# Block attention and routed experts on one core: another order of the attention steps, block means in a score bank, three subtractions on GpSimd

## The chip, the cores and the metric

The kernel runs on one core of a Trainium2 chip. Times are microseconds (us) of the device, from the first to the last instruction of the program and the little that lies around them. The engines are named as the profile names them: PE is TensorE, DVE is VectorE, ACT is ScalarE, POOL is GpSimd and SP is SyncE; PEld is PE's loading of weights.

## What is computed

```python
def _attn_ref(q, k, v):                      # 4 batches, 8 heads, 768 positions, 64 wide
    block, window = (32, 16)
    k_sum = k.reshape(B, H, nb, block, D).max(axis=3)
    v_sum = v.reshape(B, H, nb, block, D).mean(axis=3)
    scores_l = scale * np.matmul(q, k.transpose(0, 1, 3, 2))
    mask_l = np.abs(pos[:, None] - pos[None, :]) < window
    scores_s = scale * np.einsum('bhsd,bhnd->bhsn', q, k_sum) + np.log(block)
    scores_all = np.concatenate([np.where(mask_l, scores_l, -1e9), scores_s], axis=-1)
    a = np.exp(scores_all - np.max(scores_all, axis=-1, keepdims=True))
    a = a / (np.sum(a, axis=-1, keepdims=True) + 1e-09)
    return np.matmul(a, np.concatenate([v, v_sum], axis=2))

def reference(...):
    x = attention output, 3072 tokens of 512
    return _moe_ref(x, ...)                  # each token: 1 of 4 groups, 1 of its 4 experts,
                                             # relu(x @ w1) @ w2, weighted
```

Each query sees its 31 nearest keys, and 24 block keys (the maximum over 32 keys) with 24 block values (the mean over 32). The result is routed to one of 16 experts for each token.

## The kernel before

**Attention.** It runs over 16 pairs of heads, `idx` (4 pairs in each of 4 batches), and each pair has 3 steps, g = 0, 1, 2, so that step n = 3 idx + g; 48 steps in all. Every engine works through its instructions in the order in which the program is written, and that order is a table written by hand: `PLAN` (L49) lists for each g the pieces that a step is made of, and `START` (L52) the first four steps. The pieces:

- `s` (`scores`, L781): 8 fp32 matmuls of queries (64 rows) by the 120 keys of a tile, for 2 heads. PE runs them on quarters of its array, 64 by 64. Two of the three `ps_s` banks take the result. DVE adds the mask and takes the minimum (`ss`, `nm`, L795).
- `e` (L804): four exponentials on ACT, into `pr`.
- `t` (L807): four transposes of `pr` from two steps back, on the whole array into a bank of `ps_tr` (there are three); ACT copies them to `ptS` (L812).
- `v` (`values`, L815): 8 matmuls of `ptS` from three steps back with the values, on halves of the array (121 by 64), into the one bank `ps_av`; DVE divides (`rs`, `xt`, L826 and L827).
- `p0` to `p4` (`prep`, L742): for the next pair. `p0` and `p1` transpose the keys `kn` of head 0 and 1 (whole array, `ps_tr`) and copy them to `kw` in two halves (L764): the first half by ACT, the second by DVE, or by ACT too for head 1 from pair 10 on (`ACT_K1`). `p2` and `p3` transpose the queries `qn`, and ACT copies them to `qt` (L758). `p4` is DVE alone: the keys at the edges of each tile (L772, L773), the block maxima `ks` (L775), and their copy into `kw` (L778).
- `m0`, `m1` (`means`, L721): the block means of the values. `m0` is 12 matmuls with `stair` on quarters by columns (96 by 32) for the next pair, `m1` one matmul with `same` for this pair (128 by 25); both into a bank of `ps_tr`. DVE copies both (`vp` L731, `vr` L735), and POOL spreads `vr` into the values `va` (L738, six copies).
- `l0` to `l3`: transposes and matmuls (`xt`, `wcat`, 128 by 32) of the finished pair for the routing logits.
- `w`: four matmuls on zeros that keep PE busy (`keep_warm(4)`).

The scores of the next pair need all of `kw` and `qt`. Between the pieces, `advance` puts the router's small operations into DVE's stream (tokens to experts): 1 after each `s`, 2 after each `v`, 2 within `p4`, from step 17 on.

**The crossing to the experts.** Hooks in `block_attention_then_moe` start the first expert in the last steps. The first expert's weights are loaded as fp32 and split into a high part (ACT, L1035) and a low part, the difference (a DVE subtraction of 128x1024), in four pieces each for `w1` and `w2` (`split_w`, L1022). In step 47 `x_t1` transposes the first gathered tokens `xg` into two banks of `ps_tr`, from which ACT and DVE make `xT`. POOL starts the gathers of tokens and the load of `w2`. Matmuls of the experts then fill PE to the end.

Of the kernel before, what the change touches and what calls it, by code (L numbers as in the profile page):

```python
# [45 lines left out]
EPS = 1e-9  # L46
NEG = -1.0e9

PLAN = [["s", "p0", "l1", "t", "v", "p1", "e", "p4"],  # L49
        ["s", "p2", "t", "v", "m1", "l2", "e"],  # L50
        ["s", "p3", "l3", "t", "v", "l0", "m0", "e"]]
START = [["s", "e"], ["s", "m0", "e"], ["s", "w", "t", "m1", "p0", "p1", "e", "p4", "p2", "p3"],  # L52
         ["t", "v", "s", "n0", "p0", "p1", "e", "p4"]]
LAG = {"l0": 1, "l1": 2, "l2": 2, "l3": 2}

T_LAG, V_LAG = 2, 3
# [10 lines left out]
FIRST = {1: 2, 2: 1, 3: 1}  # L67

XT_AT = 4


AHEAD, LATE_AHEAD, SLOT_AHEAD, WEIGHT_AHEAD, VECTOR_NS = 300, 1500, 800, 3000, 85
# [517 lines left out]
def attention(tc, q, k, v, w_group, w_expert, ident, x_dram, ps, router, hook):  # L590
# [24 lines left out]
    with ExitStack() as st, ExitStack() as nat_st:  # L615
# [105 lines left out]
        def means(idx, part):  # L721

            va = va_ring[idx % NVA]
            t = ps_tr.next()
            if part == 0:
                for i in range(NQT):
                    j = i % 4
                    T.matmul(out=t[32 * j:32 * j + 32, 0:P], lhsT=stair[:, NBLK - 2 - 2 * i:NBLK + 30 - 2 * i],
                             rhs=va[0:KW, i, :, 0:D], start=(i < 4), stop=(i >= NQT - 4), skip_group_check=True)
                vps[idx] = sm.tile([P, P], F32, name="vp", bufs=2)  # L730
                V.tensor_copy(out=vps[idx], in_=t[:, 0:P])  # L731
            else:
                T.matmul(out=t[KW:NR, 0:P], lhsT=same, rhs=vps.pop(idx), start=True, stop=True)
                vr = wk.tile([NR, 1, 2, D], F32, name="vr")
                V.tensor_copy(out=vr[KW:NR].rearrange("p a h d -> p (a h d)"), in_=t[KW:NR, 0:P])  # L735
                n = 2
                for i in range(0, NQT, n):
                    nc.gpsimd.tensor_copy(out=va[KW:NR, i:i + n, :, 0:D], in_=vr[KW:NR].broadcast_to([NBLK + 1, n, 2, D]))  # L738


        def prep(idx, part):
# [18 lines left out]
            def put_k(h):  # L760
                rows = slice(64 * h, 64 * h + 64)
                out = kw[rows, :, 0:QT].rearrange("p t (r i j) -> p j t r i", i=4, j=2)
                for j, tv in enumerate(tr(kn, h)):
                    (nc.scalar.copy if j == 0 or h and idx in ACT_K1 else V.tensor_copy)(  # L764
                        out=out[:, j], in_=tv.rearrange("p i t r -> p t r i"))
            if part < 2:
                put_k(part)
            elif part < 4:
                put_q(part - 2)
            else:  # L770

                V.tensor_copy(out=kw[:, 1:NQT, before], in_=kw[:, 0:NQT - 1, QT - PAD:QT])  # L772
                V.tensor_copy(out=kw[:, 0:NQT - 1, behind], in_=kw[:, 1:NQT, 0:PAD])  # L773
                ks = sm.tile([P, NBLK], F32, name="ks")
                V.reduce_max(out=ks, axis=AX.X,  # L775
                             in_=kw[:, :, 0:QT].rearrange("p t (a k) -> p t a k", k=BLOCK))
                advance(OPS["k"])
                V.tensor_copy(out=kw[:, :, KW:NC], in_=ks[:, None, :].broadcast_to([P, NQT, NBLK]))  # L778
# [92 lines left out]
        NG = 3 * len(order)  # L871
        prs, pts = {}, {}

        for part in (0, 1, 4, 2, 3):
            prep(0, part)
        keep_warm(9)
        for t in prr:
# [68 lines left out]
class Experts:  # L946
# [76 lines left out]
    def split_w(self, row, which, parts, low=True, high=True):  # L1023

        raw = self.raw(row, which)
        for c in parts:
            js = slice(2 * c, 2 * c + 2)
            if which == 0:
                src = raw.rearrange("p c (j r) -> p c j r", j=FC)[:, :, js]
                h, l = (t[:, :, js] for t in self.w1s)  # L1030
            else:
                src = raw[:, js]
                h, l = (t[:, js] for t in self.w2s)
            if high:
                self.nc.scalar.copy(out=h, in_=src)  # L1035
            if low:
                self.V.tensor_tensor(out=l, in0=src, in1=h.bitcast(F32), op=ALU.subtract)

    def gather(self, row, dst, half=0):
        name, c = self.col(row, half)  # L1040
# [3 lines left out]
            in_offset=bass.IndirectOffsetOnAxis(ap=self.tabs[name, "gather"][0:dst.shape[0], c:c + 1], axis=0),  # L1044
            bounds_check=n - 1, oob_is_err=False)

    def split_t(self, cols, hi, lo, b):

        nc = self.nc
        tp = self.bank("tr", b).rearrange("p (c t) -> p c t", c=4)  # L1050
        for c in range(4):
            src = cols(c)
            self.T.transpose(out=tp[:, c].bitcast(src.dtype), in_=src, identity=self.identr if src.dtype == F32R else self.ident)
# [38 lines left out]
    def parts(self, i):  # L1092
        return [self.xT2[i % 2][:, m] for m in range(2)]

    def x_t(self, x, i):
        hi, lo = self.parts(i)
        for half in range(2):
            self.split_t(lambda c: x[half][:, c * P:(c + 1) * P], hi[:, :, half], lo[:, :, half], half)

    def x_t2(self, i):  # L1100
        if i < NPAIR:
# [162 lines left out]
        for half in range(2):  # L1264
            self.gather(("first", i + half), self.xg1[half])

    def x_t1(self):
        self.x_t(self.xg1, 0)

    def first(self):  # L1270
        for i in range(0, NE, 2):
# [68 lines left out]
def block_attention_then_moe(tc, q, k, v, w_group, w_expert, w1, w2, out):  # L1340
    nc = tc.nc
    with ExitStack() as st:
# [16 lines left out]
        def hook(n, need, advance, space):  # L1359
# [7 lines left out]
            if n == last - GATHER_AT:  # L1367
                need(2)
                ex.gather1(0)
                ex.load_w(("first", 0), 1, queue=nc.gpsimd)  # L1370
            if n == last - X_AT:
                ex.x_t1()
                if NE > 2:
                    ex.gather1(2)
            for part in range(4):
                if n == last + SPLIT_AT[part] + 1:
                    ex.split_w(("first", 0), 0, [part], high=False)
                if n == last + SPLIT_AT[part]:
                    ex.split_w(("first", 0), 0, [part], low=False)
            if n == last:  # L1380
# [68 lines left out]
```

## Time and profile before

| | us |
|---|---|
| median of 3 runs (514.64 to 517.34) | 515.81 |
| the profiled execution | 515.85 |
| its span in the trace | 514.2 |
| PE busy | 492.2 (96%) |
| DVE busy | 356.6 (69%) |
| ACT busy | 317.8 (62%) |
| POOL busy | 120.9 (24%) |

The attention loop fills the span from about 9 to 180 us; after that the experts run. The page prints the span in 40 slices. A busy share counts the time in which an engine has an instruction under way, and PE's includes time in which a started matmul waits for its turn in the array, so 96% doesn't say that PE does its work at its best rate.

### The profile page before, as it was taken

What the parts mean: (1) busy time and instruction counts of PE and PEld (TensorE: products, weight loads), DVE (VectorE), ACT (ScalarE), POOL (GpSimd) and SP (SyncE); (2) the same over time, 40 slices, a digit from 0 to 9 for tenths busy, and PEclk for the clock granted to TensorE, in tenths of its full rate; (3) what the DMA queues carried; (4) which work ended last, traced back from release to release, by engine and by line L of the source; (5) the groups of instructions that cost most, each with busy time, mean ns of one, the idle gap of its engine ahead of it and who ended that gap; (6) DMA issues with size and microseconds to landing.
All of it is one profiled execution on the core that took longest, in us unless ns stands there. A gap on an engine that the chain in (4) does not pass through costs nothing.

```text
span 514.2 us, 13346 instructions
## 1 busy us (share of the span) xinstructions
PE 492.2 (96%) x4974; PEld 415.5 (81%) x4974; DVE 356.6 (69%) x1084; ACT 317.8 (62%) x597; POOL 120.9 (24%) x205
## 2 busy tenths in 40 slices
PE   8999999999999899999999999999999999999994
PEld 4677767776777698979898989898898989897773
DVE  6687899888977978878755647483836556473773
ACT  5699888888988643216644556473645546474682
POOL 6122112211312600037020203022121202022332
PEclk9799999999999899999999999999999999999998
DMA  9999676879646820069997665665566756754891
GB/s 179 176 181 198 130 168 189 180 155 195 173 113 224 281 90 22 28 220 354 409 403 273 238 229 211 247 225 190 205 211 239 263 212 222 258 191 137 300 359 42
DMA packets 75316, 106.94 MB, mean 208 GB/s; under 512 B 40286, under 2 KB 40366, under 8 KB 75232
## 3 DMA queue, kind: packets, MB, share of 16 engines
q1 hardware_dynamic: 69184, 86.78, 58.5%
q0 software_dynamic: 6048, 19.12, 10.4%
q8 instruction: 43, 0.70, 0.6%
q14 instruction: 41, 0.34, 0.2%
HBM read 97.49 MB, written 13.24 MB: 215 GB/s over the span
## 4 chain that ended last, share of the span: by engine, by line
PE 49%; issue 19%; DMA 12%; DVE 11%; ACT 3%; POOL 3%; POOLq 1%; DVEq 0%; ACTq 0%
PE ps_s L122 26%; DMA out_dram<-y,t_unit_scatter 12%; PE ps_tr L122 12%; PE ps_av L122 10%; DVE ss L795 3%; DVE ks L775 2%; DVE kw L764 1%; ACT kw L764 1%; PE ps_lg L122 1%; POOL ohr L1042 1%; ACT qt L758 1%; PE ps_lg L662 1%; POOLq L1185 1%; ACT pr L804 1%; DVE kw L778 1%
## 5 line engine op out<-in xcount | busy, mean ns | idle before, releaser
L122 DVE TENSOR_TENSOR w2l<-w2r,w2h 128x1024 fp32r<-128x1024 f32 x52 | 63.4, 1225 | 77.1 <-ACT w2h L1035 76.6
L122 PE MATMUL ps_s<-xT,w1h 128*128 128x256 f32 x448 | 83.5, 284 | 0.0
L122 PEld LDWEIGHTS ps_s<-xT,w1h 128*128 128x128 f32 x448 | 70.7, 192 | 1.0 <-issue 0.7
L1082 POOL DMA_INDIRECT out_dram<-y,t_unit_scatter x24 | 25.7, 1069 | 190.9 <-ACT y L1077 97.7
L738 POOL COPY va<-vr 25x256 f32<-25x256 f32 x96 | 35.9, 418 | 118.8 <-DVE vr L735 118.8
L122 PE MATMUL ps_s<-xT,w1l 128*128 128x256 f32 x224 | 63.4, 283 | 0.0
L122 DVE TENSOR_TENSOR w1l<-w1r,w1h 128x1024 fp32r<-128x1024 f32 x52 | 60.4, 1219 | 3.6 <-ACT w1h L1035 3.6
L804 ACT ACTIVATE pr<-ss,nm 128x120 f32<-128x120 f32 x192 | 60.1, 387 | 3.3 <-DVE nm L795 2.9
L1120 ACT ACTIVATE hTh<-ps_s 128x512 fp32r<-128x512 f32 x48 | 28.7, 598 | 53.9 <-PE ps_s L122 31.9
L122 PE MATMUL ps_s<-ohr,w1h 128*128 128x256 f32 x320 | 58.9, 282 | 0.0
L1035 ACT CAST w2h<-w2r 128x1024 fp32r<-128x1024 f32 x52 | 53.8, 1041 | 1.5 <-DVE lg L865 0.9
L1035 ACT CAST w1h<-w1r 128x1024 fp32r<-128x1024 f32 x52 | 50.7, 1051 | 0.4 <-DMA w1r<-in_moe_w_dram 0.4
L122 PEld LDWEIGHTS ps_s<-ohr,w1h 128*128 128x128 f32 x320 | 49.8, 188 | 0.2
L122 DVE SCALAR_TENSOR_TENSOR hTl<-ps_s,hTh 128x512 fp32r<-128x512 f32 x48 | 33.2, 691 | 24.2 <-ACT hTh L1120 21.5
L795 DVE CUSTOM_DVE_ANT_0 ss<-mask,ps_s 128x120 f32<-128x120 f32 x192 | 42.1, 275 | 6.1 <-PE ps_s L122 4.6
L122 PE MATMUL ps_s<-ohr,w1l 128*128 128x256 f32 x160 | 45.0, 281 | 0.0
L122 PEld LDWEIGHTS ps_s<-xT,w1l 128*128 128x128 f32 x224 | 42.9, 192 | 0.3
L122 PE MATMUL ps_s<-kw,qt 64*64 64x120 f32 x768 | 37.5, 282 | 5.7 <-DVE nm L795 4.6
L122 PE MATMUL ps_s<-w2h,hTh 128*128 128x512 f32 x104 | 41.6, 400 | 0.0
L122 PE MATMUL ps_av<-w2h,hTh 128*128 128x512 f32 x104 | 41.6, 400 | 0.0
L122 PE MATMUL ps_av<-w2l,hTh 128*128 128x512 f32 x104 | 41.1, 395 | 0.0
L122 PE MATMUL ps_s<-w2h,hTl 128*128 128x512 f32 x104 | 41.1, 395 | 0.0
(275 smaller groups left out, 1010.6 us busy)
## 6 DMA issues: line engine op xcount, KB each, us to landing
w1r<-in_moe_w_dram SPq DMA_DIRECT2D x30, 1024.0 KB, 8.4
w2r<-in_moe_w_dram SPq DMA_DIRECT2D x28, 1024.0 KB, 5.6
kn<-in_k_dram SPq DMA_DIRECT2D x16, 384.0 KB, 4.5
qn<-in_q_dram SPq DMA_DIRECT2D x16, 384.0 KB, 5.4
va<-in_v_dram SPq DMA_DIRECT2D x32, 192.0 KB, 5.0
x_dram<-xt SPq DMA_DIRECT2D x12, 512.0 KB, 5.4
w2r<-in_moe_w_dram POOLq DMA_DIRECT2D x4, 1024.0 KB
va<-in_v_dram SPq DMA_DIRECT2D x64, 44.0 KB, 4.6
```

The source lines that it names most:

```text
L122: return f(*args, **kw)
L662: nc.tensor.matmul(out=t, lhsT=zero, rhs=zero[:, None, :].broadcast_to([P, 4, P]), start=True, stop=True)
L738: nc.gpsimd.tensor_copy(out=va[KW:NR, i:i + n, :, 0:D], in_=vr[KW:NR].broadcast_to([NBLK + 1, n, 2, D]))
L758: nc.scalar.activation(out=out[:, j], in_=tv.rearrange("p i t r -> p t i r"), func=AF.Copy, scale=-1.0 / 8.0)
L764: (nc.scalar.copy if j == 0 or h and idx in ACT_K1 else V.tensor_copy)(out=out[:, j], in_=tv.rearrange("p i t r -> p t r i"))
L775: V.reduce_max(out=ks, axis=AX.X, in_=kw[:, :, 0:QT].rearrange("p t (a k) -> p t a k", k=BLOCK))
L778: V.tensor_copy(out=kw[:, :, KW:NC], in_=ks[:, None, :].broadcast_to([P, NQT, NBLK]))
L795: V.tensor_tensor_reduce(out=ss[:, u], in0=mask[:, 1 if t == 0 else 2 if t == NQT - 2 else 0], in1=sp[h][:, j], scale=1.0, scalar=3.4e38, ...
L804: nc.scalar.activation(out=pr[:, i, 0:NC], in_=sp[:, i], func=AF.Exp, bias=nm[:, i:i + 1], scale=-1.0)
L1035: self.nc.scalar.copy(out=h, in_=src)
L1082: self.nc.gpsimd.indirect_dma_start(out=self.out, out_offset=bass.IndirectOffsetOnAxis(ap=self.tabs[name, "scatter"][0:y.shape[0], col:col ...
L1120: nc.scalar.activation(out=th[:, js], in_=hp, func=AF.Relu)
```

## The change

`PLAN` and `START` are rewritten, and seven other things go with them. In each step `t` now comes right after `s`, the transposes `p0` to `p3` stand next to it, and `v` follows. Both means stand in step g = 1 behind `v`. `p4` is cut in two: the key edges stay `p4` and move from g = 0 to g = 1, and the block maxima and their copy become `p5` in g = 2. `m0` takes a bank of `ps_s` instead of `ps_tr`. In `put_k` ACT copies both halves for head 0 and DVE both for head 1 (from pair 10 on ACT takes one of head 1's). `x_t1` takes its two banks from `ps_s`, and the low parts that DVE subtracts are issued ahead of it. Three of the eight subtractions of the first expert go to POOL (`LOW_BY_POOL`: piece 2 of `w1`, pieces 1 and 3 of `w2`). In `START` the entry `w` is written `w4`, and `w2` and `w3` are added; the loop compares with the plain `w` (L907), so none of the three issues anything.

```diff
-PLAN = [["s", "p0", "l1", "t", "v", "p1", "e", "p4"],
-        ["s", "p2", "t", "v", "m1", "l2", "e"],
-        ["s", "p3", "l3", "t", "v", "l0", "m0", "e"]]
-START = [["s", "e"], ["s", "m0", "e"], ["s", "w", "t", "m1", "p0", "p1", "e", "p4", "p2", "p3"],
-         ["t", "v", "s", "n0", "p0", "p1", "e", "p4"]]
+PLAN = [["s", "t", "p0", "p1", "v", "e"],
+        ["s", "t", "l1", "p4", "p2", "v", "m0", "l2", "m1", "e"],
+        ["s", "p5", "t", "p3", "l0", "l3", "v", "e"]]
+START = [["s", "e"], ["s", "m0", "e"], ["s", "w4", "t", "m1", "p0", "p1", "e", "p4", "p5", "p2", "w2", "p3"],
+         ["t", "v", "w3", "s", "n0", "p0", "p1", "e"], ["s", "t", "p4", "p2", "v", "m1", "e"],
+         ["s", "p5", "t", "p3", "v", "l0", "m0", "e"]]
...
+LOW_BY_POOL = ((0, 2), (1, 1), (1, 3))
...
-            t = ps_tr.next()
+            t = (ps_tr if part else ps_s).next()
...
-                    (nc.scalar.copy if j == 0 or h and idx in ACT_K1 else V.tensor_copy)(
+                    (nc.scalar.copy if h == 0 or j == 0 and idx in ACT_K1 else V.tensor_copy)(
...
-                self.V.tensor_tensor(out=l, in0=src, in1=h.bitcast(F32), op=ALU.subtract)
+                self.low(row, which, c).tensor_tensor(out=l, in0=src, in1=h.bitcast(F32), op=ALU.subtract)
+
+    def low(self, row, which, c):
+        return self.nc.gpsimd if row[0] == "first" and (which, c) in LOW_BY_POOL else self.V
...
+            for part in range(4):
+                if n == last + SPLIT_AT[part] + 1:
+                    ex.split_w(("first", 0), 0, [part], high=False)
             if n == last - X_AT:
-                ex.x_t1()
+                ex.x_t1("s")
```

On PE, step g = 0 of pair 6, from the last score matmul to the first of the next step (a row is one instruction or a run of like ones; the array's division is the whole for `kn`, `xt` and `pr`, halves for `ps_av`, quarters for `ps_s`). Before:

```order
L122 MATMUL ps_s_67<-kw_135,qt_133 64x120
L122 MATMUL ps_tr_63<-ident,kn 128x96 x4
L122 MATMUL ps_tr_64<-ident,xt_114 128x128 x2
L122 MATMUL ps_tr_65<-ident,pr_192 121x128 x4
L122 MATMUL ps_av_69<-va_110,ptS 64x65 x8
L122 MATMUL ps_tr_63<-ident,kn 128x96 x4
L122 MATMUL ps_s_68<-kw_135,qt_133 64x120
```

And now:

```order
L124 MATMUL ps_s_67<-kw_135,qt_133 64x120
L124 MATMUL ps_tr_65<-ident,pr_192 121x128 x4
L124 MATMUL ps_tr_63<-ident,kn 128x96 x4
L124 MATMUL ps_tr_64<-ident,kn 128x96 x4
L124 MATMUL ps_av_69<-va_110,ptS 64x65 x8
L124 MATMUL ps_s_66<-kw_135,qt_133 64x120
```

Both key transposes now stand beside those of `pr`, and the scores of the next step follow the values directly.

On PE, step g = 1 of the same pair, behind its score matmuls. Before:

```order
L122 MATMUL ps_tr_64<-ident,qn 128x96 x4
L122 MATMUL ps_tr_65<-ident,pr_193 121x128 x4
L122 MATMUL ps_av_69<-va_110,ptS 64x65 x8
L122 MATMUL ps_tr_63<-vp,same 25x128
L122 MATMUL ps_lg_70<-xT,wcat 32x192 x4
L122 MATMUL ps_s_67<-kw_135,qt_133 64x120
```

And now:

```order
L124 MATMUL ps_tr_65<-ident,pr_193 121x128 x4
L124 MATMUL ps_tr_63<-ident,xt_114 128x128 x2
L124 MATMUL ps_tr_64<-ident,qn 128x96 x4
L124 MATMUL ps_av_69<-va_110,ptS 64x65 x8
L124 MATMUL ps_s_68<-va_112,stair 32x128 x12
L124 MATMUL ps_lg_70<-xT,wcat 32x192 x4
L124 MATMUL ps_tr_65<-vp,same 25x128
L124 MATMUL ps_s_66<-kw_135,qt_133 64x120
```

The three groups on narrow columns (`stair`, `wcat`, `same`) now stand together, and `stair` writes the third `ps_s` bank.

On DVE, the end of step g = 0 of the same pair before, up to the next step's scores (the rows of `c` and `mx` are the router's):

```order
L764 COPY kw_136<-ps_tr_63 64x12x32
L772 COPY kw_136<-kw_136 128x11x16
L773 COPY kw_136<-kw_136 128x11x16
L775 TENSOR_REDUCE ks<-kw_136 128x24
L122 TENSOR_REDUCE mx_6_1336<-lg 128x30
L122 TENSOR_TENSOR c_6_1366<-iom_274,mx_6_1336 128x120
L778 COPY kw_136<-ks 128x12x24
L795 ISA ss,nm<-mask,ps_s_68 128x120
```

And now, in step g = 2, two steps later (`eb`, `cs`, `sb`, `seen` are the router's):

```order
L124 CAST sb_1472<-seen 128x16
L778 TENSOR_REDUCE ks<-kw_136 128x24
L124 TENSOR_REDUCE cs_1476<-eoh 128x16
L124 CAST eb_1478<-eoh 128x96
L781 COPY kw_136<-ks 128x12x24
L829 RECIPROCAL rs<-ps_av_69 128x4
L830 TENSOR_TENSOR xt_114<-ps_av_69,rs 128x2x128
L124 TENSOR_TENSOR seen<-seen,cs_1476 128x16
```

The edges, the maxima and the last copy no longer stand in one run ahead of the next step's reading of the scores; the maxima come behind the scores of step 2, and the edges stand alone in step 1.

## Rows read from the trace of the kernel before

**Rows 1.** Busy time by stretch: start:end, length, PE, PEld, DVE, ACT, POOL, clock, DMA.
```profile
35.92:65.20 29.28, 28.58 (x494) 22.36 (x494) 24.11 (x118) 26.27 (x67) 6.39 (x18) 1.00 0.93 165
65.20:96.90 31.70, 29.50 (x502) 22.70 (x501) 29.25 (x146) 26.93 (x69) 6.71 (x18) 1.00 0.77 178
96.90:106.55 9.65, 9.11 (x164) 7.25 (x163) 7.53 (x40) 8.44 (x22) 2.13 (x6) 1.00 0.70 164
106.55:169.57 63.02, 59.37 (x1007) 45.93 (x1006) 52.71 (x288) 56.42 (x144) 16.85 (x40) 1.00 0.68 174
```

**Rows 2.** PE in order of time, one pair: start, us, what, count, idle before.
```profile
49.82 0.64 PE L122 MATMUL ps_s<-kw,qt 64*64 64x120 f32 x16
50.39 0.55 PE L122 MATMUL ps_tr<-ident,kn 96*128 96x96 f32 x4
50.77 0.38 PE L122 MATMUL ps_tr<-ident,xt 128*128 128x128 f32 x2
51.00 0.60 PE L122 MATMUL ps_tr<-ident,pr 128*121 128x128 f32 x4
...
52.14 0.55 PE L122 MATMUL ps_tr<-ident,kn 96*128 96x96 f32 x4
52.62 0.64 PE L122 MATMUL ps_s<-kw,qt 64*64 64x120 f32 x16
...
55.40 0.42 PE L122 MATMUL ps_s<-kw,qt 64*64 64x120 f32 x2
56.05 0.63 PE L122 MATMUL ps_s<-kw,qt 64*64 64x120 f32 x14 [0.23 <-DVE nm L795]
56.62 0.55 PE L122 MATMUL ps_tr<-ident,qn 96*128 96x96 f32 x4
...
59.55 0.64 PE L122 MATMUL ps_s<-kw,qt 64*64 64x120 f32 x16
```

**Rows 3.** Who waited for whom, 35.92 to 158.40: us in total, times, longest.
```profile
ACT kw L764 <- PE ps_tr L122: 7.4, 13, 0.9
...
PE ps_s L122 <- DVE nm L795: 3.9, 11, 1.0
...
DVE kw L772 <- ACT kw L764: 2.6, 6, 0.7
```

**Rows 4.** PE in order of time in the first steps.
```profile
12.69 1.04 PE L662 MATMUL ps_lg<-zero 128*128 128x512 bf16 x4
...
23.16 1.08 PE L122 MATMUL ps_s<-kw,qt 64*64 64x120 f32 x16
```

**Rows 5.** Busy time around the two falls of the granted clock.
```profile
15.90:19.00 3.10, 2.16 (x26) 1.60 (x26) 2.93 (x8) 3.03 (x9) 1.18 (x4) 1.00 1.16 175
19.00:25.80 6.80, 6.65 (x71) 5.13 (x70) 3.85 (x16) 3.71 (x10) 0.00 (x0) 0.50 1.26 197
172.60:176.00 3.40, 1.92 (x18) 1.56 (x20) 2.75 (x10) 3.32 (x9) 2.72 (x6) 1.00 1.00 326
176.00:179.40 3.40, 3.40 (x44) 2.75 (x42) 3.30 (x10) 0.54 (x1) 0.61 (x1) 0.50 0.86 289
```

**Rows 6.** PE in order of time at the crossing to the experts.
```profile
175.22 0.70 PE L122 MATMUL ps_tr<-ident,pr 128*121 128x128 f32 x4 [1.20 <-DVE xT L122]
...
177.95 1.14 PE L122 MATMUL ps_av<-va,ptS 121*64 121x65 f32 x16
...
179.65 0.38 PE L122 MATMUL ps_s<-xT,w1h 128*128 128x256 f32 x1
```

**Rows 7.** ACT in order of time at the same place.
```profile
175.95 0.59 ACT L812 COPY ptS<-ps_tr 121x512 f32<-121x512 f32 x1
```

**Rows 8.** DVE in order of time near the end of attention.
```profile
170.61 1.23 DVE L122 TENSOR_TENSOR w1l<-w_first,w1h 128x1024 fp32r<-128x1024 f32 x1
...
173.41 0.44 DVE L122 TENSOR_SCALAR lo_first<-t_first_gather 128x4 int32<-128x4 int32 x1
```

**Rows 9.** POOL in order of time at the same place.
```profile
170.64 3.18 POOL L738 COPY va<-vr 25x256 f32<-25x256 f32 x6 [1.08 <-DVE vr L735]
```

More of the change, by code (lines that the diff above doesn't have):

```diff
@@ L769, in prep @@
                 put_q(part - 2)
-            else:
+            elif part == 4:
                 V.tensor_copy(out=kw[:, 1:NQT, before], in_=kw[:, 0:NQT - 1, QT - PAD:QT])
                 V.tensor_copy(out=kw[:, 0:NQT - 1, behind], in_=kw[:, 1:NQT, 0:PAD])
+            else:
                 ks = sm.tile([P, NBLK], F32, name="ks")
@@ L872, in attention @@
         prs, pts = {}, {}
-        for part in (0, 1, 4, 2, 3):
+        for part in (0, 1, 4, 5, 2, 3):
             prep(0, part)
@@ L1045, in gather, with split_t @@
             bounds_check=n - 1, oob_is_err=False)
-    def split_t(self, cols, hi, lo, b):
+    def split_t(self, cols, hi, lo, b, bank="tr"):
         nc = self.nc
-        tp = self.bank("tr", b).rearrange("p (c t) -> p c t", c=4)
+        tp = self.bank(bank, b).rearrange("p (c t) -> p c t", c=4)
         for c in range(4):
@@ L1093, in parts, with x_t @@
         return [self.xT2[i % 2][:, m] for m in range(2)]
-    def x_t(self, x, i):
+    def x_t(self, x, i, bank="tr"):
         hi, lo = self.parts(i)
         for half in range(2):
-            self.split_t(lambda c: x[half][:, c * P:(c + 1) * P], hi[:, :, half], lo[:, :, half], half)
+            self.split_t(lambda c: x[half][:, c * P:(c + 1) * P], hi[:, :, half], lo[:, :, half], half, bank)
     def x_t2(self, i):
@@ L1265, in gather1, with x_t1 @@
             self.gather(("first", i + half), self.xg1[half])
-    def x_t1(self):
-        self.x_t(self.xg1, 0)
+    def x_t1(self, bank="tr"):
+        self.x_t(self.xg1, 0, bank)
     def first(self):
@@ L1375, in hook @@
             for part in range(4):
-                if n == last + SPLIT_AT[part] + 1:
-                    ex.split_w(("first", 0), 0, [part], high=False)
                 if n == last + SPLIT_AT[part]:
```

## The prediction

> **What bounds the kernel now.** I read the busy times by stretch first, then PE in order of time over one pair of heads, then the list of waits, and then the places that the change touches at the start and at the crossing to the experts. The change touches nothing behind the first expert, so the question is how much earlier the experts begin.
>
> The 13 pairs from 35.92 to 169.57 us take 133.65 us [rows 1]. In the first and third stretch (4 pairs, 38.93 us, where the router gives DVE little) PE is busy nearly all the time: 28.58 of 29.28. But that is more than it needs. In the pair from 49.82 to 59.55, 9.73 us, the last scores take from 55.40 to 56.62, 1.22 us, where the first take 0.57 (49.82 to 50.39) [rows 2]: two of 16 records start, then PE waits for a score bank that DVE hasn't read. So 0.65 us is a wait, and PE needs 9.08. Behind that wait is one chain within step 0 and step 1: the second key transpose stands behind the values, ACT waits for it (7.4 us in 13 waits), DVE's edges wait for ACT's copy (2.6), edges, maxima and copy follow in one run, and DVE comes late to the scores (PE's 3.9 us in 11 waits) [rows 3]. In the second and fourth stretch the router's operations load DVE: 29.25 of 31.70, and 52.71 of 63.02, with ACT at 56.42 of 63.02 [rows 1]. There three engines stand near their limits.
>
> **Changes of the array's division.** I price one from [rows 2]. Four key transposes take 0.48 us to the next start with a change behind them (52.14 to 52.62) and 0.38 with none behind (50.39 to 50.77): 0.10 for the end. Two transposes of `xt`, with no change on either side, take 0.23 (50.77 to 51.00), so 0.115 for 128 columns, 0.086 for 96, 0.345 for four; the 0.38 holds 0.035 for the beginning. A change costs about 0.14 us. By the tables, a pair has 4 + 4 + 5 = 13 of them before (a step: scores, whole, values, whole, scores; in step 2 the narrow `m0` besides), and 3 + 4 + 3 = 10 now. So PE needs 3 x 0.14 = 0.42 less for a pair: 8.66.
>
> **What the loop can then be.** PE's saving is worth only what the next engine leaves. The number of copies on ACT and DVE is the same, they only change places. By stretch the largest of the three needs is: first, ACT 26.27 (PE 3 x 8.66 = 25.98); second, DVE 29.25; third, PE 8.66 (ACT 8.44); fourth, ACT 56.42 (PE 6 x 8.66 = 51.96 and some router matmuls) [rows 1]. Together 120.6 us, 13.05 below the 133.65 of now. That is the end at which no engine ever waits for another. At the other end each pair keeps a wait as large as the 0.65 of now: 13 x 0.65 = 8.45 back, a gain of 4.6. I take a wait of 0.4 for a pair, a gain of 13.05 - 5.2 = 7.85. My reason for a value nearer to the old wait than to none: the chain behind the 0.65 is cut in three (keys in step 0, edges in step 1, maxima in step 2, each a step before its reader), but the work per step is uneven. Step 1 gets `m0`'s 12 matmuls on PE besides what it has, while ACT's load is largest in step 2, and ACT will be what is late next. `m0` in a score bank leaves the two score banks of the next step free, since there are three; DVE reads it before the step is over. `m1` comes later in step 1, behind `m0` and `l2`, so `vr` and POOL's six copies (2.13 us in a pair [rows 1]) start about 1 us later; the values that need them come two steps on, and there behind the key transposes, so I cost that at nothing. If that cover is gone it is up to 1 us a pair, inside the lower end.
>
> **The start.** The four warming matmuls (1.04 us [rows 4], 0.87 to the next start at 13.56) go, because `w4`, `w2` and `w3` issue nothing. The transposes behind them start earlier, and with them the chain of key copies: 0.9 us of gain, between 0 (ACT holds it up) and 1.04. What it may cost is the clock. Between 19.0 and 25.8 the granted clock is 0.50, the 1.2 GHz level, after a stretch in which PE was busy 2.16 of 3.10 us [rows 5]. Score matmuls of half a step take 1.08 at that level [rows 4] and 0.64 at the upper [rows 2], so 41% of such a stretch is lost: 2.8 of 6.8 us. The new start may lose that once more, or never fall. I take no change, with both ends, -2.8 and +2.8.
>
> **The crossing.** PE waits 1.20 us for a `ps_tr` bank that DVE frees only behind `xT` [rows 6]; with `xT` in `ps_s` banks the transposes of `pr` don't wait for it. Next late is ACT's copy `ptS`, begun at 175.95 and done at 176.54 [rows 7]; the values that read it start at 177.95 now [rows 6], so at most 1.4 us is won ahead of the first expert matmul at 179.65, and up to 0.5 more if the fall of the clock at 176.0 (PE busy 1.92 of 3.40 before it [rows 5]) goes. I take 1.0, between 0 and 1.9.
>
> **Subtractions on POOL.** DVE loses 3 x 1.23 = 3.7 us of work [rows 8], but none of the three is on the path: expert matmuls already run back to back there. The trace has no such subtraction on POOL. Its copies of 256 columns take 2.13 / 6 = 0.355 [rows 1], so 1024 columns with one input would be 1.4 us and with two inputs read in turn 2.8, an estimate from that row. Nearest is the two-input end, 2.8. The first layer reads its piece 2 only behind half of its matmuls, and the second layer its pieces 1 and 3 behind 6 and 18 of its 24, so other work lies over them, and I put 0 on the path, between -0.5 and +3. Each engine pays for the other, though: while DVE's subtraction ran at 170.61, POOL's six copies took 3.18 instead of 2.13 [rows 8, 9], and DVE's `lo_first`, 4 columns, took 0.44 and ended at 173.85 as those copies ended at 173.82.
>
> The Trainium skill, SBUF — State Buffer, section "SBUF: two separate sides", speaks against this edit: the port pair that DVE and GpSimd share is an exclusive lock held for a whole instruction, by DVE operations with two SBUF inputs too. The rows of 170.61 and 173.41 agree. The skill's GPSIMD Engine Reference, section "Elementwise — side-by-side cycle accounting", gives 4.5 us for 2048 fp32 columns of a two-input operation, so an estimate of 2.25 for 1024; by that the sum stays as it is.
>
> **The sum.** The profiled execution took 515.85 us, 514.2 of it span, and the median of the runs is 515.81, so the terms go straight off the median: 0.9 + 7.85 + 1.0 = 9.75, and 515.8 - 9.75 = 506.1 us.
>
> **Rivals.** *The wait is only moved.* Three transposes now follow each other into three `ps_tr` banks, and each bank is freed by ACT or DVE; PE waits there instead of for the score bank. For it: ACT's share, 56.42 of 63.02. Against: `pr` and `ptS` have a step of slack. The loop gives 4.6 and the crossing nothing: 515.8 - 0.9 - 4.6 = 510.3.
>
> *Slower: the clock falls in the loop.* PE's need drops to 8.66 in pairs that DVE or ACT hold at 9.5 to 10, so it idles where now it is nearly always busy, in step 0 and 2 above all. Both falls of now came after such idling [rows 5]. A fall of 3.4 us costs 1.4; one in each of the 9 pairs of the second and fourth stretch costs 12.6: 506.1 + 12.6 = 518.7. It decides from 7 falls on (9.75 / 1.4). Against it: those stretches stand at 1.00 with PE busy 29.50 of 31.70.
>
> *POOL's subtractions come late.* If one takes 2.8 and waits for DVE's lock, the second layer waits for its low parts, 1 us for each of three: 509.
>
> *The change doesn't do what it says.* The rows of PE show the fewer changes; only the warming entries are without effect, which is in the sum.
>
> **How the numbers follow.** Forecast 0.60 (503 to 509); wait only moved 0.17; POOL late 0.08; nearly no waits left, 0.06 (515.8 - 0.9 - 13.05 - 1.9 = 500); the clock, 0.09. The range runs from 502.0 to 513.0: below, between the forecast and the case without waits; above, the moved wait and one more stretch of low clock at the start (510.3 + 2.8 = 513.1). About 0.5%, 2.6 us, is what a measurement of this kernel can tell. Faster than 513.2: 0.60 + 0.17 + 0.08 + 0.06 less some of the moved wait with a cold start, 0.86; within, 0.06; slower, 0.08.
>
> **What would show it.** A pair without router work should take 8.9 to 9.2 us, one with it 9.5 to 10.1. The waits of ACT for key transposes and of DVE's edges for ACT should be gone, and the scores' wait small. The key groups should cost no more than 0.38 with a transpose behind. The first expert matmul should come at about 170. I am wrong if pairs still take 9.7, if the clock's row shows halves inside the loop, or if the start's low stretch grows.

## The result, and the profile after

The changed kernel takes 520.41 us, the median of four executions (517.02 to 522.49), against 515.22 for the kernel before in the same session: a ratio of 1.0079, 95% interval 1.0050 to 1.0108. It is slower. The forecast was 506.1, with a range of 502.0 to 513.0.

The profiled execution took 517.02 us, 515.4 of it span. It is the fastest of the four: the granted clock, as a mean over the span, was 0.993 in it and 0.982 to 0.985 in the others. So two things are to be explained: 1.2 us against the profiled execution of before (where 9.75 less was forecast), and 3.4 us more in the usual execution.

By milestone, in the two profiled executions (starts of score matmuls and of the first expert matmul):

| | before | after | gain | forecast gain |
|---|---|---|---|---|
| scores of step 8 begin | 35.92 | 35.68 | 0.24 | 0.9 |
| 13 pairs, to the scores of step 47 | 133.65 | 130.85 | 2.80 | 7.85 |
| from there to the first expert matmul | 10.08 | 11.12 | -1.04 | 1.0 |
| from there to the end of the span | 334.6 | 337.8 | -3.2 | 0 |
| sum | | | -1.2 | 9.75 |

**The loop.** Busy time by stretch, after: start and end, length, PE, PEld, DVE, ACT, POOL, granted clock, DMA. The four stretches hold the same pairs as [rows 1].

```profile
35.68:63.02 27.34, 26.65 (x494) 22.24 (x493) 23.14 (x117) 24.16 (x63) 6.39 (x18) 1.00 1.08 176
63.02:92.78 29.76, 27.44 (x500) 22.32 (x499) 27.65 (x143) 26.85 (x72) 6.39 (x18) 1.00 0.82 188
92.78:102.91 10.13, 9.13 (x166) 7.38 (x165) 7.81 (x42) 8.05 (x21) 2.13 (x6) 1.00 0.80 185
102.91:166.53 63.62, 55.77 (x982) 44.21 (x982) 52.31 (x282) 55.41 (x143) 16.50 (x40) 1.00 0.68 169
```

Two of the cuts of [rows 1], at 65.20 and 96.90, stand a little behind the start of the scores, which begin at 65.14 and at 96.51:

```profile
96.51 0.41 PE L122 MATMUL ps_s<-kw,qt 64*64 64x120 f32 x2
```

By the starts of the scores the four stretches of before are 29.22, 31.37, 10.04 and 63.02 us, so the first six pairs gain 1.88 and 1.61 us, the seventh loses 0.09, and the last six, which take 63.62, lose 0.60. The prediction's needs with its wait of 0.4 us for a pair make 27.47, 30.45, 9.06 and 58.82: the first six pairs beat that by 0.8 us, and the whole shortfall of the loop lies in the last seven, 1.07 us in the first of them and 4.80 in the other six. In the last six no engine is busier than before, DVE 52.31 against 52.71 and ACT 55.41 against 56.42, and the clock is full. The time is waits. Who waited for whom, 35.68 to 155.57 (us in total, times, longest):

```profile
DVE kw L766 <- ACT kw L766: 9.0, 6, 1.8
...
PE ps_s L124 <- DVE kw L781: 7.1, 12, 1.1
```

All six of the first kind are copies for the keys of pairs 10 to 15, one for each pair (up to 1.8 us); the first, at 99.57, already lies in the third stretch. DVE and ACT in order of time, one such place. DVE:

```profile
131.25 0.56 DVE L766 COPY kw<-ps_tr 64x384 f32<-64x384 f32 x1 [0.96 <-ACT kw L766]
131.85 0.18 DVE L829 RECIPROCAL rs<-ps_av 128x4 f32<-128x4 f32 x1
```

ACT:

```profile
129.65 1.57 ACT L766 COPY kw<-ps_tr 64x384 f32<-64x384 f32 x3
```

ACT now makes three of the four key copies in one run, 129.65 to 131.22; DVE's one, the second half of head 1, waits for ACT's first half of the same rows, and the division of the values (`rs`) and the next scores' `ss` are queued behind it on DVE. Both halves come from one `ps_tr` bank and go, interleaved, to the same rows of `kw`; which of the two makes DVE wait is not shown.

**The crossing.** PE in order of time:

```profile
172.70 0.69 PE L124 MATMUL ps_av<-va,ptS 121*64 121x65 f32 x16 [0.92 <-DVE jb_first L124]
177.02 0.70 PE L124 MATMUL ps_lg<-xT,wcat 128*32 128x192 f32 x8 [3.63 <-DVE xT L851]
177.65 0.58 PE L124 MATMUL ps_s<-xT,w1h 128*128 128x256 f32 x1
```

The 1.20 us of [rows 6] are gone and the values of step 46 come at 172.70, but then PE waits 3.63 us for a copy on DVE. DVE in order of time, from the first operation of the router's last round to the copy:

```profile
174.25 0.27 DVE L124 TENSOR_REDUCE mx<-lg 128x30 f32<-128x120 f32 x1
...
176.45 0.18 DVE L124 TENSOR_TENSOR seen<-seen,cs 128x16 f32<-128x16 f32 x1
176.54 0.42 DVE L851 COPY xT<-ps_tr 128x256 f32<-128x256 f32 x1
```

The copy belongs to `l1`, which the new table has in step 49 instead of 48. The hook of step 48 puts the last low part of `w1` (1.21 us from 172.65) and all waiting router operations into DVE's stream, so they now stand ahead of it, and DVE does them back to back. At the end of the wait the clock falls. Busy time by stretch (columns as above):

```profile
173.40:177.00 3.60, 0.00 (x0) 0.00 (x0) 3.36 (x16) 0.78 (x2) 2.46 (x2) 1.00 0.74 242
177.25:180.66 3.41, 3.41 (x22) 3.01 (x15) 0.26 (x1) 0.00 (x0) 0.00 (x0) 0.50 0.58 220
```

PE stands still for 3.6 us while DVE is busy for 3.36 of them; then, with PE at work again, the granted clock is 0.50, the 1.2 GHz level. The kernel before has a fall at this place too, of 3.40 us [rows 5].

**The start.** PE in order of time:

```profile
18.14 1.17 PE L124 MATMUL ps_s<-kw,qt 64*64 64x120 f32 x16 [0.70 <-DVE kw L781]
19.66 0.98 PE L124 MATMUL ps_s<-va,stair 96*32 96x128 f32 x24 [0.35 <-DMA va<-in_v_dram]
21.01 0.88 PE L124 MATMUL ps_tr<-ident,kn 96*128 96x96 f32 x8 [0.37 <-DMA kn<-in_k_dram]
...
34.23 0.87 PE L124 MATMUL ps_s<-va,stair 96*32 96x128 f32 x21 [1.22 <-DMA va<-in_v_dram]
```

The scores of step 3 are earlier (18.14 against 18.70), but `m0`, a step earlier too, waits for the load of the values, and the next keys for theirs. The longest of these waits is the last. The scores of step 7 begin at 30.57, 2.57 us earlier than before, but between them and those of step 8 `m0`, which stood in step 8 before, waits 1.22 us for the values of the next pair, and step 8 begins only 0.24 earlier. The rest of the difference is mainly the work that step 1 of a pair now has more.

**The subtractions on POOL.** POOL, then DVE at the same time:

```profile
170.27 2.37 POOL L1040 TENSOR_TENSOR w1l<-w_first,w1h 128x1024 fp32r<-128x1024 f32 x1
...
190.93 4.84 POOL L1040 TENSOR_TENSOR w2l<-w2r,w2h 128x1024 fp32r<-128x1024 f32 x2 [14.76 <-ACT w2h L1038]
```

```profile
191.32 2.19 DVE L124 TENSOR_TENSOR dd<-lg,mx 128x120 f32<-128x120 f32 x1
193.54 2.37 DVE L124 SCALAR_TENSOR_TENSOR c<-dd,iom 128x120 f32<-128x120 f32 x1
...
197.06 1.22 DVE L124 TENSOR_TENSOR w2l<-w2r,w2h 128x1024 fp32r<-128x1024 f32 x1
```

One takes about 2.4 us on POOL. Meanwhile two router operations of DVE with two inputs in SBUF, 0.28 us each at other places, last until POOL's end; DVE's own `w2l` is late, and PE waits for it (below).

### The profile page after: what moved, and what is told of

Same layout as the page of the kernel before. It is cut to its first block, busy times and chain, and to the rows that moved or that the text cites. A ratio compares the mean times of both kernels' runs of the same rounds, so it can differ in the third digit from the quotient of the medians.

```text
span 515.4 us, 13357 instructions
## 1 busy us (share of the span) xinstructions
PE 482.6 (94%) x4970; PEld 412.6 (80%) x4970; DVE 353.7 (69%) x1081; ACT 314.6 (61%) x597; POOL 128.2 (25%) x208
## 4 chain that ended last, share of the span: by engine, by line
PE 67%; DVE 17%; DMA 8%; ACT 3%; issue 3%; SPq 2%; POOL 0%; ACTq 0%; POOLq 0%; DVEq 0%
PE ps_s L124 45%; PE ps_av L124 15%; PE ps_tr L124 6%; DVE ss L798 3%; DMA va<-in_v_dram 2%; DVE ks L778 2%; DMA x_dram<-xt 2%; PE ps_lg L124 2%; DMA w1r<-in_moe_w_dram 2%; DMA kn<-in_k_dram 2%; DVE xt L830 1%; SPq L649 1%; ACT kw L766 1%; DVE w1l L124 1%; ACT pr L807 1%
## 5 line engine op out<-in xcount | busy, mean ns | idle before, releaser
L124 DVE TENSOR_TENSOR w2l<-w2r,w2h 128x1024 fp32r<-128x1024 f32 x50 | 61.1, 1225 | 77.1 <-ACT w2h L1038 76.1
L124 PE MATMUL ps_s<-xT,w1h 128*128 128x256 f32 x448 | 84.8, 287 | 0.0
L124 PEld LDWEIGHTS ps_s<-xT,w1h 128*128 128x128 f32 x448 | 71.8, 194 | 1.1 <-issue 0.8
L740 POOL COPY va<-vr 25x256 f32<-25x256 f32 x96 | 34.6, 405 | 115.4 <-DVE vr L737 114.3
L124 PE MATMUL ps_s<-w2l,hTh 128*128 128x512 f32 x104 | 41.1, 395 | 0.0
```

The lines of the kernel that those rows point to most:

```text
L124: return f(*args, **kw)
```

## The experiments

The theories. **A**: three places of the changed order itself cost the gain: `l1` behind the router's operations at the crossing, the key maxima `p5` read by the very next scores, and the subtractions on POOL. **C**: the clock, which falls at the start because `w4`, `w2` and `w3` issue nothing. **D**: in pairs with router work DVE and ACT are simply full, and a wait taken away comes up elsewhere. **E**, formed after the first runs: in pairs 10 to 15 DVE stands behind ACT's key copies. **P**: POOL's subtractions are a relief that DVE needs. **R**: DVE has the router's work to do at the crossing either way. Medians, and ratios to the kernel before in the same session:

| run | edit | median us | ratio (95%) |
|---|---|---|---|
| a_again | none | 520.33 | 1.0070 (1.0044 to 1.0096) |
| a_warm | warming entries issue | 517.23 | 1.0015 (0.9993 to 1.0036) |
| a_low_dve | no subtraction on POOL | 518.95 | 1.0053 (1.0025 to 1.0081) |
| a_l1_back | `l1` in step 48 | 513.89 | 0.9951 (0.9928 to 0.9975) |
| a_p5_early | `p5` in step 1 | 518.69 | 1.0051 (1.0028 to 1.0075) |
| a_l1_warm | `l1`, warming | 512.90 | 0.9937 (0.9917 to 0.9957) |
| a_l1_warm_low | `l1`, warming, no POOL | 512.14 | 0.9934 (0.9906 to 0.9963) |
| b_l1_late | kernel before, `l1` in step 49 | 522.42 | 1.0105 (1.0066 to 1.0144) |
| c_putk | a_l1_warm_low, key copies as before | 509.95 | 0.9866 (0.9826 to 0.9907) |
| c_k1dve | a_l1_warm_low, `ACT_K1` empty | 509.86 | 0.9869 (0.9826 to 0.9913) |
| c_k1dve_p5 | c_k1dve, `p5` in step 1 | 511.41 | 0.9914 (0.9876 to 0.9952) |
| c_best | a_l1_warm_low, key copies mixed | 510.75 | 0.9869 (0.9832 to 0.9906) |

**a_again.** The changed kernel itself.

> The changed kernel once more, unchanged, to see how its time spreads. Theory A (three waits of its own order cost the gain: maxima read at once, router work ahead of the copy of xT at the crossing, the lock by GpSimd's subtractions): about 1.2 us slower than before whenever the clock falls no more often than in its profiled execution (ratio 1.003), and any further time comes with a lower mean clock. Rival C (the clock): the median is 4 to 5 us above before (ratio 1.008 to 1.01), and the mean granted clock is 0.985 or lower where the profiled execution had 0.993.

Eight executions, 517.77 to 520.68, mean clock 0.983 to 0.992; 520.33 in the middle. The profiled one, 517.90 at 0.992, has no fall at the start, so the median contains a loss that neither profile of this kernel shows. Both theories expected a longer time to come with a lower mean clock. It alone doesn't account for the times: two executions at 0.990 and 0.991 took 520.36 and 520.30, and one at 0.987 took 517.77.

**a_warm.** The entries do what they say.

```
-                elif step == "w":
-                    keep_warm(4)
+                elif step[0] == "w":
+                    keep_warm(int(step[1:]))
```

> The entries w4, w2 and w3 issue their 9 warming matmuls (2.3 us of PE at most). Rival C: without them the clock falls at the start in most executions; with them the stretch of low clock at the start is gone or no longer than 3.4 us and the median is 2 to 4 us below the changed kernel's (516.5 to 518.5). Theory A: the start is bound by the key copies and loads, the 9 matmuls cost up to 1 us and the clock is what it was: 519 to 522.

517.23, 3.1 below a_again. In all 12 executions the mean clock is 0.990 to 0.993. Where the time is lost without the matmuls is seen in two other runs whose start is the changed kernel's: a_low_dve and a_p5_early. Busy time by stretch, a_low_dve, then a_p5_early:

```profile
18.00:20.69 2.69, 1.78 (x27) 1.31 (x29) 2.41 (x7) 2.59 (x7) 0.63 (x2) 1.00 1.03 239
20.69:30.93 10.24, 10.24 (x108) 7.90 (x109) 5.51 (x33) 5.33 (x14) 1.42 (x4) 0.50 1.29 180
```

```profile
12.00:18.39 6.39, 5.28 (x68) 3.89 (x60) 4.93 (x22) 5.42 (x15) 2.43 (x7) 1.00 1.36 132
18.39:25.21 6.82, 6.55 (x70) 5.13 (x69) 3.52 (x21) 3.00 (x9) 0.00 (x0) 0.50 1.29 192
```

The start runs 10.24 or 6.82 us at half the clock in some executions of the same instructions, and none in others: so it is in two of the five profiled executions without the matmuls, and in none of the seven with them (c_best has a fall later, after 37 us). In a_p5_early the scores of step 8 then begin at 36.72, 1.0 us later than in the profiled execution of after: those of step 7 are 1.9 late, but the wait of `m0` that follows shrinks from 1.22 to 0.38. In a_low_dve they begin at 39.54, 3.9 us later, of which 1.9 stand there already in the scores of step 2, ahead of the fall. In a_warm PE is busy there for 3.32 of 3.50 us, in the profiled execution of after 2.40:

```profile
16.00:19.50 3.50, 3.32 (x35) 1.84 (x33) 3.25 (x8) 3.40 (x10) 1.32 (x4) 1.00 1.14 177
```

```profile
16.00:19.50 3.50, 2.40 (x37) 1.64 (x36) 2.61 (x8) 3.13 (x8) 0.67 (x2) 1.00 1.13 188
```

C holds for the start as far as the fall goes: with the matmuls it isn't there. That the fall makes up the whole 3.1 us isn't shown, since these two traces put about 1.0 and 1.9 us on it; whether late loads lengthen other executions was not tested. The matmuls themselves delay the start by 0.27 us (scores of step 4 at 22.09 against 21.82).

**a_low_dve.**

```
-LOW_BY_POOL = ((0, 2), (1, 1), (1, 3))
+LOW_BY_POOL = ()
```

> All eight subtractions on DVE again. Theory A: DVE's two router operations of 2.2 and 2.4 us at 191 to 196 us shrink to 0.3 each, PE's wait of 1.0 us for w2l goes, and the second half of the first expert begins 1 us earlier: 1 to 2 us below the changed kernel. Rival P (GpSimd does them in free time and DVE needs the relief): no difference within 0.5 us, or up to 1 us slower since DVE does 3.7 us more ahead of the expert.

518.95, 1.4 below a_again, with intervals that overlap; its mean clocks, 0.974 to 0.987, are lower than a_again's, so the two medians differ by more than this edit. The mechanism is as A had it: the two stretched operations are short again, and PE's wait for `w2l` is gone. DVE in a_low_dve, then PE's wait after 186 us in the changed kernel, which a_low_dve doesn't have:

```profile
201.28 0.28 DVE L124 TENSOR_TENSOR dd<-lg,mx 128x120 f32<-128x120 f32 x1
201.59 0.28 DVE L124 SCALAR_TENSOR_TENSOR c<-dd,iom 128x120 f32<-128x120 f32 x1
```

```profile
PE ps_av L124 <- DVE w2l L124: 1.0, 1, 1.0
```

The size, about 1 us, can't be told from none by the times alone.

**a_l1_back.** In the last steps the tokens' second half stands in step 48 again (lines of this and later kernels with this edit are one higher).

```
+LAST = {48: ["l1", "t", "v"], 49: ["t", "v", "l2"]}
-            for step in START[n] if n < len(START) else PLAN[g]:
+            for step in START[n] if n < len(START) else LAST.get(n, PLAN[g]):
```

> In the last steps alone the second half of the tokens' transposes (l1) stands in step 48 again, ahead of the router's operations. Theory A: PE's wait of 3.63 us for DVE's copy xT at 177.0 goes, the clock doesn't fall at 177.25, and the first expert matmul comes 3 to 4 us earlier: 3 to 4 us below the changed kernel. Rival R (DVE must do the same router work ahead of the expert's low parts either way): the wait moves to the ranks or to w2l, and the time is within 1 us of the changed kernel's.

513.89, 6.4 below a_again, and faster than the kernel before. PE in order of time, then the whole of attention's end and the first expert in busy time by stretch:

```profile
172.96 0.69 PE L125 MATMUL ps_av<-va,ptS 121*64 121x65 f32 x16 [1.15 <-DVE hi_first L125]
...
174.04 0.39 PE L125 MATMUL ps_s<-xT,w1h 128*128 128x256 f32 x1
```

```profile
166.25:174.04 7.79, 6.49 (x101) 5.20 (x100) 7.24 (x25) 6.28 (x14) 6.36 (x9) 1.00 0.92 313
174.04:190.00 15.96, 15.41 (x147) 14.31 (x144) 13.06 (x43) 8.51 (x15) 4.31 (x3) 1.00 0.36 128
```

The wait for `xT` at this place is gone, the clock stays full, and the first expert matmul comes 7.79 us after the scores of step 47, where it was 11.12. A holds here and R falls: the router's operations fit behind the copy, beside the expert's matmuls. The gain is larger than A's 3 to 4 us. The traces show 3.3 us ahead of the first expert matmul and 1.3 in the matmuls behind it, which run at the full clock (2.97 against 4.30 us, below); the rest of the 6.4 isn't traced.

**b_l1_late.** The same in the other direction, on the kernel before.

```
+LAST = {48: ["t", "v"], 49: ["l1", "t", "v", "l2"]}
```

> The kernel before, with l1 alone put into step 49 in its last steps, behind the router's operations of step 48. Theory A: the same wait of 3 to 4 us for xT appears ahead of the first expert matmul, less the 1.2 us that PE waits there before: 2 to 4 us slower than before, 518.5 to 521 us. Rival (the wait needs the rest of the new table, whose values are earlier there): within 1 us of before.

522.42, 6.3 above the kernel before in its session (516.09), more than was expected. PE in order of time, and two stretches:

```profile
178.72 0.69 PE L123 MATMUL ps_av<-va,ptS 121*64 121x65 f32 x16 [1.08 <-DVE xt L828]
183.01 0.87 PE L123 MATMUL ps_lg<-xT,wcat 128*32 128x192 f32 x8 [3.60 <-DVE xT L849]
```

```profile
172.00:181.64 9.64, 5.10 (x72) 3.99 (x70) 9.08 (x31) 5.79 (x13) 6.08 (x8) 1.00 0.77 277
181.64:188.47 6.83, 5.46 (x30) 4.87 (x31) 1.79 (x9) 0.31 (x1) 0.00 (x0) 0.50 0.28 105
```

The wait of 3.6 us comes with this one move, without anything else of the change, and the stretch of low clock at this place, 3.40 us in the kernel before [rows 5], is twice as long with it. The move alone is as large as the whole loss of the changed kernel.

**a_p5_early.**

```
-        ["s", "t", "l1", "p4", "p2", "v", "m0", "l2", "m1", "e"],
-        ["s", "p5", "t", "p3", "l0", "l3", "v", "e"]]
+        ["s", "t", "l1", "p4", "p5", "p2", "v", "m0", "l2", "m1", "e"],
+        ["s", "t", "p3", "l0", "l3", "v", "e"]]
```

> The key maxima and their copy (p5) stand in step 1 behind the edges, a step ahead of the scores that read them, as the prediction had said of them. Theory A: PE's waits of 7.1 us in 12 for that copy go, and the pairs with router work take 9.6 to 10 us: 3 to 4 us below the changed kernel in the loop, so 516 to 518 us. Rival D (in those pairs DVE and ACT are simply full, and the wait only changes its name): the loop from step 8 to step 47 stays within 1 us, 519 to 521 us.

518.69, between what A and what D expected, with an interval that overlaps that of a_again. The wait for the maxima is gone and the loop is not shorter: scores of step 8 to step 47, 131.45 us (36.72 to 168.17) against 130.85. PE's waits in the late pairs, where the changed kernel has `PE ps_s <- DVE kw`:

```profile
PE ps_tr L124 <- DVE vr L737: 2.8, 4, 1.0
...
PE ps_tr L124 <- DVE bo_first L124: 0.9, 1, 0.9
```

They only have another name. A falls for `p5`. DVE is late as a whole there, but D isn't the answer either, since DVE is busy 52.31 of 63.62 us. What makes it late is the 9.0 us above; hence E.

**a_l1_warm, a_l1_warm_low.** The edits above together.

> l1 back in step 48, and the 9 warming matmuls issued. Theories A and C together: no fall of the clock at the start nor at the crossing in nearly all executions, mean clock 0.995 or more, 511 to 512.5 us with little spread. Rival (the warming matmuls cost as much as the clock gives back): 513.5 to 515 us, as with l1 alone.

> As the one before, and all eight subtractions on DVE. Theory A: the wait of 1.4 us for w2l and the 4 us of the two stretched router operations go: 1 to 1.5 us below that one, 509.5 to 511.5 us. Rival P (DVE is late for the experts without GpSimd's help): equal, or up to 2 us above it.

512.90 with 12 executions between 512.12 and 514.58, mean clock 0.994 to 0.998, and 512.14, each some tenths above the range that was expected. The two gains, by `l1` and by the warming matmuls, overlap: 6.4 and 3.1 apart, 7.4 together. Without POOL 0.8 less, again below what the intervals tell apart, though from the first expert matmul to the end the profiled execution takes 334.9 us where a_l1_back takes 336.9.

**c_putk, c_k1dve.** Only the shares of the key copies differ from a_l1_warm_low. First:

```
-(nc.scalar.copy if h == 0 or j == 0 and idx in ACT_K1 else V.tensor_copy)(
+(nc.scalar.copy if j == 0 or h and idx in ACT_K1 else V.tensor_copy)(
```

> As a_l1_warm_low (512.1 us), with the key copies shared out as in the kernel before: of head 0 and of head 1 the first half by ACT, the second by DVE, from pair 10 on both of head 1 by ACT. Theory E (in pairs 10 to 15 DVE's copy of the second half stands behind ACT's copy of the first, and waits 1.5 us in each, 9.0 us in all, and everything behind it on DVE with it): that wait goes to where it was, below 0.5 us a pair, and the six late pairs take 0.3 to 0.8 us less each: 508 to 510.5 us. Rival D (DVE and ACT are full there): within 1 us, and the wait comes up elsewhere.

Second:

```
-ACT_K1 = range(10, B * NP)
+ACT_K1 = ()
```

> As a_l1_warm_low, with ACT_K1 empty: in every pair ACT copies both halves of head 0 and DVE both of head 1, so that no half waits for the other engine. DVE has 0.55 us more in each of the six late pairs and ACT 0.55 less. Theory E: the 9.0 us of DVE's waits for ACT's copy go, the late pairs take 9.6 to 10.1 us instead of 10.1 to 10.95: 507.5 to 510 us. Rival D: DVE's added 3.3 us of work cost as much as the wait did: 511.5 to 513 us.

509.95 and 509.86, each 2.2 below a_l1_warm_low, which ran in another session; by the ratios to the kernel before it is 3.5 us, and in the profiled executions the 13 pairs take 127.86 and 127.12 us instead of 130.86. Of each the first and the last stretch, c_putk, then c_k1dve:

```profile
36.22:64.83 28.61, 27.24 (x493) 22.40 (x492) 23.10 (x118) 24.53 (x65) 6.42 (x18) 1.00 1.00 167
...
104.99:164.08 59.09, 54.28 (x983) 44.39 (x982) 51.71 (x281) 55.08 (x141) 15.85 (x40) 1.00 0.70 181
```

```profile
36.37:63.70 27.33, 26.64 (x493) 22.24 (x493) 23.14 (x117) 24.17 (x64) 6.39 (x18) 1.00 1.09 180
...
103.01:163.49 60.48, 54.62 (x983) 44.36 (x982) 54.79 (x286) 52.13 (x136) 15.78 (x40) 1.00 0.67 175
```

The last six pairs fall from 63.6 to 59.09 and 60.48, with the same work on DVE and ACT in c_putk and with 2.5 us more on DVE in c_k1dve. E holds and D falls. In c_putk the first three pairs pay 1.27 us for it, 9.54 a pair instead of 9.11: there the old shares make DVE wait (2.9 us in three). Each share is best in one half of the loop.

**c_k1dve_p5.** c_k1dve with the two lines of a_p5_early.

> As c_k1dve, and the key maxima in step 1 as in a_p5_early. If p5's place costs something once DVE no longer stands behind ACT, the loop is 1 to 3 us shorter than in c_k1dve: 505.5 to 508.5 us. If the wait for the maxima only shows that DVE is late, as a_p5_early says so far, it is within 1 us of c_k1dve.

511.41; the loop takes 127.77 us against 127.12. The place of `p5` costs nothing even where DVE no longer stands behind ACT.

**c_best.**

```
+(nc.scalar.copy if (h or j == 0 if idx in ACT_K1 else h == 0) else V.tensor_copy)(
```

> As a_l1_warm_low, with the key copies shared out by pair: up to pair 9 as in the changed kernel (ACT both halves of head 0, DVE both of head 1), from pair 10 on as in the kernel before (DVE only the second half of head 0). If the early pairs keep their 9.11 us (a_l1_warm_low) and the late ones the 59.1 us for six of c_putk, the loop from step 8 to step 47 takes 126.0 to 126.6 us and the kernel 508 to 509 us. If the two shares disturb each other where they meet, it stays at the 509.9 us of c_putk and c_k1dve.

510.75, a ratio of 0.9869 like c_putk and c_k1dve: not the 508 to 509 that were expected. The shares do not disturb each other; the early pairs take 9.11 and the last six 59.38:

```profile
38.42:48.48 10.06, 10.06 (x166) 8.52 (x165) 7.77 (x39) 7.71 (x20) 2.13 (x6) 0.88 1.21 172
48.48:66.70 18.22, 17.75 (x330) 14.81 (x329) 15.44 (x78) 16.44 (x44) 4.26 (x12) 1.00 0.98 169
106.00:165.38 59.38, 54.38 (x983) 44.39 (x982) 51.85 (x281) 54.92 (x141) 15.80 (x40) 1.00 0.69 179
```

But the granted clock fell in the first pair here, which costs it 0.95 us, and again at the crossing. The first of these falls comes behind the wait of `m0` for the values, longer here than in the other traces:

```profile
36.51 0.87 PE L125 MATMUL ps_s<-va,stair 96*32 96x128 f32 x21 [1.94 <-DMA va<-in_v_dram]
```

Which execution falls where varies, so three kernels near 510 can't be ranked. All three are 1.3% faster than the kernel before, and 2% faster than the changed one by way of the ratios to the kernel before.

## Why the prediction was wrong

- **What bounds the kernel: right, with wrong sizes.** Where no router work stands, a pair was to take 8.66 + 0.4 = 9.06; it takes 9.11. The parts differ. PE's need fell from 9.08 to 9.11 - 0.23 = 8.88 (0.23 is the wait left, in the rows below), so three changes of division are worth 0.20, about 0.07 each, not 0.14. The rest of the gain is the wait that went. PE in order of time, after, the groups of step 0 and the start of the next pair:

```profile
38.57 0.68 PE L124 MATMUL ps_s<-kw,qt 64*64 64x120 f32 x16 [0.23 <-DVE kw L781]
39.18 0.70 PE L124 MATMUL ps_tr<-ident,pr 128*121 128x128 f32 x4
39.72 0.83 PE L124 MATMUL ps_tr<-ident,kn 96*128 96x96 f32 x8
40.48 0.69 PE L124 MATMUL ps_av<-va,ptS 121*64 121x65 f32 x16
...
47.68 0.69 PE L124 MATMUL ps_s<-kw,qt 64*64 64x120 f32 x16 [0.23 <-DVE kw L781]
```

  The eight key transposes take 0.76 instead of 0.38 + 0.48, so 0.10 is won at one place, and the group of `pr` behind the scores takes 0.54 where it took 0.52 behind `xt` (51.00 to 51.52). Pricing one end and one beginning and taking all changes to be alike was too much.
- **The loop's floors: the step that failed first.** "The number of copies on ACT and DVE is the same, they only change places" was true of the number. But a copy's place also sets for whom its engine stands still. For the last six pairs the working gave 56.42 + 6 x 0.4 = 58.8; the kernel took 63.62, and with the old shares c_putk took 59.09. So the floor by busy time and the leftover wait come out for these pairs once no copy of DVE stands behind three of ACT: some 4.5 us in the profiled loop, and 0.6 in the pair ahead (10.13 against 9.55). That they come out is in part chance, since in c_putk the same shares cost 1.27 us in the first pairs. The working did say that ACT would be late next, but looked for it in step 2; it was late in step 0, with the keys.
- **"A step before its reader"** was false for the maxima: the scores right behind step 2 read them, and PE is seen waiting 7.1 us. It cost nothing by itself (a_p5_early, c_k1dve_p5).
- **The crossing: the larger failure.** The working took "next late is ACT's copy `ptS`" from [rows 6, 7] and looked only at the bank that the change had set free. `l1` moving from step 48 to 49 was read as part of the loop, where it has a step to spare. The prediction had not named what the hook of step 48 puts onto DVE between the two places. Forecast: 1.0 us won; measured: 1.04 lost ahead of the first expert matmul, and about 1.3 more by the clock behind it (its first 24 matmuls take 177.65 to 181.95, 4.30 us; in a_l1_back 174.04 to 177.01, 2.97). In medians the move is worth 6.4 (a_l1_back) and 6.3 (b_l1_late).
- **The start: the ends were right, the value not.** Little was won by leaving out the matmuls (0.24 of 0.9: loads are late next, not copies), and "the new start may lose that once more" is what two of the five traces with this start show. The clock was put at 0 between -2.8 and +2.8; with the matmuls back the median is 3.1 us lower (a_warm). A fall of 6.82 us cost 1.0 by step 8 and not 2.8, since the wait for the load behind it covers a part.
- **POOL.** Estimated 2.8 us for one, measured 2.37 to 2.44. The rows of 191.32 and 193.54 fit the lock that the working described, and the second layer waited 1.0 us for a low part: inside the term's bounds, and one of the three waits of "1 us" that the rival named. The times don't tell it from nothing.
- **"The change touches nothing behind the first expert"** put a term at nothing, and the traces contradict it. From the first expert matmul to the end, 334.6 us became 337.8; with `l1` back it is 336.9, and with POOL's subtractions gone too and the warming matmuls in, 334.9 (a_l1_warm_low).
- **The rivals.** "Slower: the clock falls in the loop" had the right sign by a wrong place: the clock is 1.00 in all four stretches of the loop. In the traces it falls at the crossing, in some at the start, and in c_best in the loop's first pair, but not in the pairs that DVE or ACT hold. "The wait is only moved" came nearest for the loop, 2.80 us against its 4.6, but PE waits there for the copy of the maxima and not for `ps_tr` banks.

**What adds up.** The forecast missed by 14.3 us (520.4 - 506.1). Putting `l1` back and letting the warming entries issue gives 7.4 (a_l1_warm), the subtractions 0.8, the copies' shares 2.2: 10.4, and the kernel stands at 510. Of the remaining 4 us the profiled execution of c_k1dve (508.62) places 2.5: against the kernel before it loses 0.45 at the start, gains 6.53 in the loop (7.85 forecast) and 1.58 at the crossing (1.0 forecast), and loses 0.5 behind it. The other 1.2 us, from there to the median, are not traced.

## What to carry to other kernels

When a step moves in an order written by hand, look at every place where the table runs with different neighbours, the last rounds above all, and list what other code puts into the same engine's stream between the old place and the new. A floor from busy time holds only if no engine's instruction stands behind another engine's queue, so when work of the same amount changes engines, follow each copy's wait and what is queued behind it. Where filler work keeps PE busy, taking it away is priced by the times and granted clocks of many executions, not by one profile. And a piece of work that moves a step ahead needs its loads a step earlier too.

## What the runs showed of the hardware

- A wait of 3.6 us on PE was followed by low clock each time: in b_l1_late and in the changed kernel the granted clock fell to 0.50 at its end, for 6.83 and 3.41 us, and in a_l1_back, with a wait of 1.15 us there, it didn't fall. In the kernel before, with one of 1.20, it fell for 3.40.
- The same instructions at the start got the full clock in one execution and half of it for 6.8 or 10.2 us in another (a_again against a_p5_early and a_low_dve); with PE busy 3.32 of 3.50 us there, none of 12 executions had a mean clock below 0.990.
- A subtraction of 128x1024 takes 2.4 us on POOL and 1.22 on DVE, and DVE's operations of 128x120 with two SBUF inputs took 2.19 and 2.37 us beside it instead of 0.28, in the changed kernel and again in a_l1_back.
